# Where a float64 conversion on VectorE keeps its intermediate words: SBUF or a PSUM bank

## The chip, the cores and the metric

One core of one Trainium2 chip runs the whole program. The metric is device time in microseconds, the median of three runs. Engines by their short names: PE (TensorE matmul; PEld its weight load), DVE (VectorE), ACT (ScalarE), POOL (GpSimd), SP (SyncE, which issues most DMAs).

## The reference

Three stages follow one another. The first is attention over 2 batches, 8 heads, 768 positions and 64 columns: each query sees the keys less than 16 positions away and one summary (maximum of the keys, mean of the values) of each block of 32. The second is a dense layer with a gated activation, the third a layer of 8 experts in which every token goes to one expert by a greedy assignment with equal capacity.

```python
scores = concat(where(|i - j| < 16, scale * q @ k.T, -1e9), scale * q @ k_sum.T + log(32))
x = softmax(scores) @ concat(v, v_sum)          # per head, then [1536, 512]
h = x @ w_in                                    # [1536, 2048]
y = (h * clip(h + 3, 0, 6) / 6) @ w_out         # [1536, 512]
assigned = greedy(argsort(-(y @ w_gate)))       # 192 tokens to each of 8 experts
out[mask_e] = relu(y[mask_e] @ w1[e]) @ w2[e]
```

The weights `w_in` and `w_out` reach the core as float64, the rest as float32.

## The kernel before, in words

The 1536 tokens are 12 tiles of 128; three tiles make a unit, so there are four units of 384. Every large matmul runs three times, with operands split into a high part in the fp32r form and the remainder (`WH`, `WL`, `XH`, `XL`).

A float64 weight tile of 128 x 512 arrives as pairs of 32-bit words. DVE turns it into float32 with three integer instructions (`f32_ops`): shift and mask of the upper word, the sign bits or-ed in, the upper bits of the lower word or-ed in. All three write the target tile, and the second and third also read it. For `w_in` these are 16 tiles (`w_conv`, recorded under L268, with the target `win32`, four buffers), for `w_out` again 16 (`fold_take`, under L529, with the target `wout32`, three buffers). Then `w_split` follows: ACT copies the tile into `WH` (L285), POOL subtracts to get `WL` (L286). After its third step a conversion lets SP load the tile four (`w_in`) or two (`w_out`) further on.

`drive` merges generators into one program order by planned shares. Engines run their queues in that order, and semaphores hold an instruction until its operands are there. The stretches in time: a prologue with the attention of unit 0 and the first conversions; layer one of unit 0 (`gemm1`) beside the attention of unit 1 and the other `w_in` conversions; layer one of units 1 and 2 beside the attention of the next unit; layer one of unit 3 beside the `w_out` conversions and their transposes (`out_slice`, `fold_take`, `fold`, which fold the gate's weights into `w_out`); the second layer (`gemm2`) beside the routing; the experts.

PSUM has eight banks, named by number in `bank(i)`. Layer one puts each of the 16 groups of a unit (12 matmuls into one bank, lines 587 to 589) into banks 5 and 6 in turn, and for unit 3 into 5, 6, 2, 3. ACT reads the bank (L590), and then DVE's gate (L601) reads it; after that the bank is free. `turn` transposes the attention weights of a half tile (4 heads), the first half of a tile into bank 2, the second into bank 3 (L404), and ACT copies them out (L406). The preparation of the keys uses banks 2 and 3 as well. In the attention, DVE's small instructions (L382, L394) and its copies of key windows (L354 to L360) have inputs and outputs in SBUF; POOL scales the weights (L396).

The gate of a group is put into the program order after the next group, and behind any conversion that this next group brings.

Of the kernel before, what the change touches and what calls it, by code (L numbers as in the profile page):

```python
# [10 lines left out]
I32 = mybir.dt.int32  # L11
AF = mybir.ActivationFunctionType
OP = mybir.AluOpType
# [14 lines left out]
NU = NT // UT  # L28
U = UT * 128
# [58 lines left out]
def build(ctx, tc, q, k, v, w_in, w_out, w_gate, w1, w2, out):  # L88
    nc = tc.nc
    PE, ACT, DVE, POOL, SP = nc.tensor, nc.scalar, nc.vector, nc.gpsimd, nc.sync  # L90
# [28 lines left out]
    def bank(i):  # L119
        return psum.tile([128, 512], FT, name=f"bank{i}")  # L120
# [107 lines left out]
    win64 = [conv.take([2 * 512], I32) for _ in range(4)]  # L228
    win32 = [conv.take([512]) for _ in range(4)]
    NW = len(win64)  # L230
    wi, wo = w_in.bitcast(I32), w_out.bitcast(I32)

    def f32_ops(dst, src):


        w = src.rearrange("p (f t) -> p f t", t=2)
        d = dst.bitcast(I32)
        return [partial(DVE.tensor_scalar, d, w[:, :, 1], 3, 0x3FFFFFF8, op0=OP.logical_shift_left, op1=OP.bitwise_and),
                partial(DVE.scalar_tensor_tensor, d, w[:, :, 1], -0x40000000, d, op0=OP.bitwise_and, op1=OP.bitwise_or),
                partial(DVE.scalar_tensor_tensor, d, w[:, :, 0], 29, d, op0=OP.logical_shift_right, op1=OP.bitwise_or)]  # L240

    def w_in_load(s):
        SP.dma_start(win64[s % NW].rearrange("p (k f) -> p k f", k=KD),
# [20 lines left out]
            loaded[0] += 1  # L264

    def w_conv(s):
        for op in f32_ops(win32[s % 4], win64[s % NW]):
            op()  # L268
            yield
        if s + NW < NF:  # L270
            soon.append(partial(w_in_load, s + NW))
# [127 lines left out]

    def turn(n, h):  # L400
        A = Abuf[(2 * n + h) % (LAG + 1)]
        p = bank(2 + h)
        for c in range(4):
            PE.transpose(p[:KEYS, c * 128:(c + 1) * 128], A[:, c], ident)  # L404
        at = att.tile([128, 4, 128], FT, name="at", bufs=2)
        ACT.activation(at[:KEYS], p[:KEYS].rearrange("p (c s) -> p c s", c=4), AF.Copy)  # L406
        ats[n, h] = at
# [35 lines left out]
    def halves():  # L443
        for n in range(NT):
# [9 lines left out]
            for h in range(2):  # L454
                t = pend.pop(0) if len(pend) >= LAG else None
                if t:
                    turn(*t)
                    turned.append(t)
                    yield 660
# [26 lines left out]
            if i == 5:  # L486
                while pend or turned:
                    if turned:
                        yield 700
                        values(*turned.pop(0))  # L490
                        yield 1000
                        emit_x()
                    if pend:
                        yield 800
                        t = pend.pop(0)
                        turn(*t)
                        turned.append(t)
                        yield 660
# [26 lines left out]
        SP.dma_start(wout64[f % 2], wo[f * 128:(f + 1) * 128, :])  # L525

    def fold_take(f):
        for op in f32_ops(wout32[f % 3], wout64[f % 2]):
            op()  # L529
        if f + 2 < NF:  # L530
            soon.append(partial(fold_load, f + 2))
# [34 lines left out]
    def out_slice():  # L566

        f = taken[0]
        taken[0] += 1
        if f + 1 < NF:  # L570
            fold_take(f + 1)
        w_split(NF + f, POOL)
        if f % FG == FG - 1:
            fold_pair(f // FG)
# [4 lines left out]
    def gemm1(u, first=False):  # L579
        if u < NU - 1:  # L580
            T[u] = tpool.tile([128, NF, U], FT, name="t")
        xh, xl = (t[u][:, :KD * U].rearrange("p (k s) -> p k s", k=KD) for t in (XH, XL))
        for f in range(NF):
            p = bank((5, 6, 2, 3)[f % (4 if u == NU - 1 else 2)])[:, :U]
            wh, wl = (t[f].rearrange("p (k f) -> p k f", k=KD) for t in (WH, WL))
            for kk in range(KD):
                PE.matmul(p, wh[:, kk, :], xh[:, kk, :], start=kk == 0, stop=False)  # L587
                PE.matmul(p, wh[:, kk, :], xl[:, kk, :], start=False, stop=False)  # L588
                PE.matmul(p, wl[:, kk, :], xh[:, kk, :], start=False, stop=kk == KD - 1)  # L589
            ACT.activation(T[u][:, f, :], p, AF.Relu, bias=three)  # L590
            soon.append(partial(gate, T[u][:, f, :], p))
            if u == NU - 1:
                if (f + 1) * (NF - LEFT) // NF > taken[0]:
                    out_slice()
                if f == EARLY:
                    next(second)
            yield 1950
# [169 lines left out]
    def splits():  # L767
        for s in range(NF + CLAG):
            if s < NF:
                for _ in w_conv(s):  # L770
                    yield 1
            if s >= CLAG:
                w_split(s - CLAG, POOL)
            yield 1
# [4 lines left out]
    for u in range(NU):  # L779
        st = []  # L780
        if u + 1 < NU:
            st = [[attend_unit(u + 1), ATTS[u + 1], -0.02, END[u]]]
            if u == 0:
                st.append([splitting, 4 * (NF - AHEAD) + CLAG, 0.0, S1])
        else:
            actx.close()
            tlast = ctx.enter_context(tc.tile_pool(name="tlast", bufs=1))
            late = ctx.enter_context(tc.tile_pool(name="late", bufs=1))
            T[u] = tlast.tile([128, NF, U], FT, name="t")
            big = late.tile([128, 2 * 2 * 512], I32)  # L790
            wout64 = [big[:, i * 1024:(i + 1) * 1024] for i in range(2)]
            fa = xpool.tile([128, KD * U + 12], FT, name="x")
            wout32 = [fa[:, i * 512:(i + 1) * 512] for i in range(3)]
            fb = xpool.tile([128, KD * U + 12], FT, name="x")
            wt = fb[:, :KD * FG * 128].rearrange("p (k j f) -> p k j f", k=KD, j=FG)
            woy = fb[:, KD * FG * 128:(KD + 1) * FG * 128]
            wg = fb[:, (KD + 1) * FG * 128:(KD + 1) * FG * 128 + KD * 32].rearrange("p (k e) -> p k e", k=KD)
            for f in range(2):
                fold_load(f)
            POOL.memset(wg, 0.0)  # L800
            SP.dma_start(wg[:, :, :E], w_gate.rearrange("(k p) e -> p k e", p=128))
            fold_take(0)
        drive([[gemm1(u), G1, 0, 1]] + st, soon)
# [418 lines left out]
```

## Time and profile before

| | |
|---|---|
| median of three runs | 602.12 us (601.99 to 603.04) |
| the profiled execution | 600.1 us, its span 598.2 us |
| mean granted TensorE clock | 0.981 of full speed |
| PE busy | 551.2 us (92% of the span) |
| DVE busy | 400.6 us (67%) |
| ACT busy | 288.8 us (48%) |
| POOL busy | 178.2 us (30%) |
| chain that ended last | PE 39%, issue 27%, DVE 23%, DMA 4% |

Shares of the whole span are averages over stages that have different limits, so they are a start only. The chain is followed back from the last instruction: its share for DVE is time in which DVE's work was what the next step waited for. The table by stretches of time tells which engine is full where, and the waits tell for whom an engine stood still.

### The profile page before, as it was taken

The page shows a single profiled execution, that of the slowest core. Times are in us where ns is not written, and L with a number is a line of the kernel's source. Part 1 is how long each engine was busy: PE and PEld are TensorE (multiplying, and loading weights), DVE is VectorE, ACT ScalarE, POOL GpSimd, SP SyncE. Part 2 cuts the span into 40 slices and gives each one's busy share as a digit, 9 for nine tenths or more (in the row PEclk, how much of TensorE's full clock was granted, in tenths as well). Part 3 has the DMA queues.
Part 4 walks back from the last instruction along what each step waited for, and adds up shares of the span by engine and source line. Part 5 has one row for each costly group of instructions (what it writes and reads, how often), then busy time and mean ns, then how long its engine had stood idle before and what let it go on. Part 6 is the DMA issues. An engine that isn't in the chain of part 4 may idle for free.

```text
span 598.2 us, 10910 instructions
## 1 busy us (share of the span) xinstructions
PE 551.2 (92%) x3811; PEld 466.8 (78%) x3811; DVE 400.6 (67%) x1215; ACT 288.8 (48%) x694; POOL 178.2 (30%) x204
## 2 busy tenths in 40 slices
PE   7679778989999999899999898899999999999994
PEld 6558667878899999776687676678789889988883
DVE  6898994555534399961037787762588888888880
ACT  4376453435645455641131131133577677776760
POOL 1444648111111034662243434545101101110111
PEclk9879998989999999999999999999999999999998
DMA  9985981202210245330060000003579879887811
GB/s 204 253 194 147 257 200 33 49 18 64 58 39 1 72 142 175 112 93 1 1 201 11 0 2 2 0 19 142 168 219 283 231 241 283 265 253 240 253 61 32
DMA packets 102400, 75.06 MB, mean 125 GB/s; under 512 B 47488, under 2 KB 88448, under 8 KB 101952
## 3 DMA queue, kind: packets, MB, share of 16 engines
q1 hardware_dynamic: 100352, 67.96, 41.8%
q0 software_dynamic: 1984, 6.32, 2.9%
q8 instruction: 32, 0.52, 0.4%
q14 instruction: 32, 0.26, 0.1%
HBM read 67.55 MB, written 6.71 MB: 124 GB/s over the span
## 4 chain that ended last, share of the span: by engine, by line
PE 39%; issue 27%; DVE 23%; DMA 4%; POOL 3%; ACT 2%; SPq 1%; POOLq 0%; ACTq 0%; DVEq 0%
PE bank L587 7%; PE bank L588 6%; PE bank L589 6%; DVE t L268 5%; PE bank L704 3%; PE bank L705 3%; PE bank L706 3%; DVE big L889 3%; POOL out_dram L1025 2%; PE bank L894 2%; DVE x L529 2%; PE bank L613 2%; DMA t<-in_q_dram 2%; PE bank L419 1%; DVE A L380 1%
## 5 line engine op out<-in xcount | busy, mean ns | idle before, releaser
L587 PE MATMUL bank<-x,wh 128*128 128x384 f32 x256 | 92.4, 361 | 9.5 <-DVE t L601 9.3
L295 DVE TENSOR_TENSOR wl<-t,wh 128x1024 fp32r<-128x1024 f32 x64 | 77.0, 1221 | 20.5 <-ACT wh L294 18.1
L681 ACT ACTIVATE work<-t 128x384 fp32r<-128x384 f32 (+2 forms) x80 | 36.4, 459 | 107.5 <-PE bank L705 101.2
L589 PE MATMUL bank<-x,wl 128*128 128x384 f32 x256 | 87.4, 341 | 0.8 <-POOL wl L286 0.8
L588 PE MATMUL bank<-x,wh 128*128 128x384 f32 x256 | 87.1, 340 | 0.8 <-DVE x L77 0.8
L590 ACT ACTIVATE t<-bank,three 128x384 f32<-128x384 f32 x64 | 37.2, 581 | 94.1 <-PE bank L589 94.0
L682 POOL TENSOR_TENSOR tlx<-t,work 128x384 fp32r<-128x384 f32 (+1 forms) x52 | 56.8, 1094 | 84.2 <-ACT work L681 84.2
L704 PE MATMUL bank<-wh,work 128*128 128x512 f32 x192 | 78.0, 406 | 2.0 <-DVE t L601 2.0
L706 PE MATMUL bank<-wh,tlx 128*128 128x512 f32 x192 | 75.3, 392 | 0.1
L705 PE MATMUL bank<-wl,work 128*128 128x512 f32 x192 | 74.8, 390 | 0.0
L1050 PE MATMUL bank<-x,wh 128*128 128x384 f32 x256 | 73.7, 360 | 0.5 <-DVE x L976 0.5
L294 ACT ACTIVATE wh<-t 128x1024 fp32r<-128x1024 f32 x64 | 65.6, 1047 | 0.0
L1052 PE MATMUL bank<-x,wl 128*128 128x192 f32 x256 | 64.2, 251 | 0.0
L601 DVE SCALAR_TENSOR_TENSOR t<-t,bank 128x384 f32<-128x384 f32 x64 | 34.7, 548 | 40.0 <-ACT t L590 40.0
L396 POOL TENSOR_TENSOR A<-A,sm 128x480 f32<-128x480 f32 x24 | 24.2, 1010 | 119.0 <-ACT at L406 74.9
L587 PEld LDWEIGHTS bank<-x,wh 128*128 128x128 f32 x256 | 48.9, 191 | 13.4 <-DVE t L601 5.9
L1025 POOL DMA_INDIRECT out_dram<-t,idx x16 | 14.9, 930 | 141.6 <-DVE t L1074 136.1
L588 PEld LDWEIGHTS bank<-x,wh 128*128 128x128 f32 x256 | 49.1, 192 | 1.4 <-DVE x L77 1.4
L589 PEld LDWEIGHTS bank<-x,wl 128*128 128x128 f32 x256 | 48.9, 191 | 1.2 <-POOL wl L286 1.2
L1052 PEld LDWEIGHTS bank<-x,wl 128*128 128x128 f32 x256 | 48.9, 191 | 0.3
L1066 PE MATMUL bank<-wh,t 128*128 128x512 f32 x128 | 49.0, 392 | 0.0
L1050 PEld LDWEIGHTS bank<-x,wh 128*128 128x128 f32 x256 | 48.1, 188 | 1.2 <-DVE x L976 0.8
(182 smaller groups left out, 1088.9 us busy)
## 6 DMA issues: line engine op xcount, KB each, us to landing
t<-in_moe_w_dram SPq DMA_DIRECT2D x128, 256.0 KB
t<-in_moe_w_in_dram SPq DMA_DIRECT2D x16, 512.0 KB
big<-in_moe_w_out_dram SPq DMA_DIRECT2D x16, 512.0 KB
VW<-in_v_dram SPq DMA_DIRECT2D x20, 192.0 KB
t<-in_v_dram SPq DMA_DIRECT2D x4, 768.0 KB
t<-xs SPq DMA_DIRECT2D x8, 258.0 KB
raw<-in_q_dram SPq DMA_DIRECT2D x8, 256.0 KB
t<-in_k_dram SPq DMA_DIRECT2D x12, 128.0 KB
```

The costliest lines, as they stand in the source:

```text
L294: ACT.activation(hi, x, AF.Copy)
L295: DVE.tensor_tensor(lo, x, hi.bitcast(FT), op=OP.subtract)
L587: PE.matmul(p, wh[:, kk, :], xh[:, kk, :], start=kk == 0, stop=False)
L588: PE.matmul(p, wh[:, kk, :], xl[:, kk, :], start=False, stop=False)
L589: PE.matmul(p, wl[:, kk, :], xh[:, kk, :], start=False, stop=kk == KD - 1)
L682: (DVE if placed[0] else POOL).tensor_tensor(ths[i][1], t, ths[i][0].bitcast(FT), op=OP.subtract)
L704: PE.matmul(acc[j], th[:, c], WH[s], start=f == 0, stop=False)
L705: PE.matmul(acc[j], th[:, c], WL[s], start=False, stop=False)
L706: PE.matmul(acc[j], tl[:, c], WH[s], start=False, stop=f == NF - 1)
L1050: PE.matmul(p, a[:, kk, :], xt[:, kk].rearrange("p c s -> p (c s)"), start=kk == 0, stop=False, skip_group_check=True)
L1052: PE.matmul(p[:, :CAP], b[:, kk, :], xt[:, kk, 0, :], start=False, stop=kk == KD - 1, skip_group_check=True)
L1066: PE.matmul(p, x, w, start=m == 0 and i == 0, stop=m == NM - 1 and i == 2)
```

## The change

The helper `f32_ops` takes a third argument, a bank of PSUM. The first two steps write their words there, the second and third read them from there, and only the third writes the target. Both users pass bank 3. To free that bank, `turn` uses bank 2 for both halves, and layer one of unit 3 rotates over banks 5, 6, 2. Nothing else differs; the same instructions are issued on the same engines in the same order.

```diff
-    def f32_ops(dst, src):
+    def f32_ops(dst, src, mid):
...
-        d = dst.bitcast(I32)
+        o, d = dst.bitcast(I32), mid.bitcast(I32)
         return [partial(DVE.tensor_scalar, d, w[:, :, 1], 3, 0x3FFFFFF8, op0=OP.logical_shift_left, op1=OP.bitwise_and),
                 partial(DVE.scalar_tensor_tensor, d, w[:, :, 1], -0x40000000, d, op0=OP.bitwise_and, op1=OP.bitwise_or),
-                partial(DVE.scalar_tensor_tensor, d, w[:, :, 0], 29, d, op0=OP.logical_shift_right, op1=OP.bitwise_or)]
+                partial(DVE.scalar_tensor_tensor, o, w[:, :, 0], 29, d, op0=OP.logical_shift_right, op1=OP.bitwise_or)]
...
-        for op in f32_ops(win32[s % 4], win64[s % NW]):
+        for op in f32_ops(win32[s % 4], win64[s % NW], bank(3)):
...
-        p = bank(2 + h)
+        p = bank(2)
...
-        for op in f32_ops(wout32[f % 3], wout64[f % 2]):
+        for op in f32_ops(wout32[f % 3], wout64[f % 2], bank(3)):
...
-            p = bank((5, 6, 2, 3)[f % (4 if u == NU - 1 else 2)])[:, :U]
+            p = bank((5, 6, 2)[f % (3 if u == NU - 1 else 2)])[:, :U]
```

## Rows read from the trace of the kernel before

**Rows 1.** Busy us by stretch: length, PE, PEld, DVE, ACT, POOL, clock, DMA, GB/s.
```profile
50.00:95.00 45.00, 34.81 (x302) 30.60 (x294) 43.03 (x97) 23.14 (x65) 24.06 (x17) 1.00 0.77 178
95.00:208.00 113.00, 110.61 (x942) 100.51 (x941) 51.14 (x212) 54.55 (x165) 23.79 (x25) 0.97 0.18 43
208.00:250.00 42.00, 42.00 (x284) 39.98 (x287) 37.79 (x56) 22.55 (x44) 18.02 (x14) 1.00 0.43 145
250.00:265.00 15.00, 12.20 (x83) 9.25 (x81) 13.58 (x16) 7.67 (x16) 11.70 (x13) 1.00 0.41 124
265.00:430.00 165.00, 156.67 (x928) 119.18 (x928) 87.03 (x377) 46.85 (x98) 64.54 (x79) 1.00 0.14 46
```

**Rows 2.** PE's waits, 60 to 100, then 250 to 300: total us, times, longest.
```profile
PE bank L587 <- DVE t L601: 9.3, 6, 2.6
...
PE bank L704 <- DVE t L601: 2.0, 1, 2.0
PE bank L539 <- DVE wgo L553: 0.8, 1, 0.8
```

**Rows 3.** Stretches, DVE's conversions alone (L268 twice, then L529): busy, clock, DMA, GB/s.
```profile
24.00:50.00 26.00, 9.06 (x13) 0.87 0.88 210
50.00:95.00 45.00, 29.39 (x35) 1.00 0.77 178
...
208.00:253.00 45.00, 33.95 (x39) 1.00 0.42 145
```

**Rows 4.** Single lines of the kernel: duration in ns, shortest/median/longest; starts; shapes.
```profile
L268 DVE SCALAR_TENSOR_TENSOR t<-t x32: 662/692/1708, 25.4 to 93.1; 128x512 int32<-128x512 int32 x32
L268 DVE TENSOR_SCALAR t<-t x16: 396/416/1506, 25.0 to 89.5; 128x512 int32<-128x512 int32 x16
...
L601 DVE SCALAR_TENSOR_TENSOR t<-t,bank x64: 536/547/556, 50.4 to 253.4; 128x384 f32<-128x384 f32 x64
```

**Rows 5.** Timeline, POOL and then DVE, 89 to 93 us: start, duration, instruction.
```profile
89.03 4.82 POOL L286 TENSOR_TENSOR wl<-t,wh 128x512 fp32r<-128x512 f32 x3
...
89.54 1.51 DVE L268 TENSOR_SCALAR t<-t 128x512 int32<-128x512 int32 x1
91.08 1.63 DVE L268 SCALAR_TENSOR_TENSOR t<-t 128x512 int32<-128x512 int32 x1
92.64 0.54 DVE L601 SCALAR_TENSOR_TENSOR t<-t,bank 128x384 f32<-128x384 f32 x1
```

**Rows 6.** DVE's groups by line and shape: busy us, mean ns | idle before.
```profile
L682 DVE TENSOR_TENSOR tlx<-t,work 128x256 fp32r<-128x256 f32 x12 | 5.0, 424 | 8.7 <-ACT work L681 8.7
L202 DVE COPY VW<-bank 24x512 f32<-24x512 f32 x8 | 5.1, 689 | 2.3 <-PE bank L198 2.3
L885 DVE SCALAR_TENSOR_TENSOR bank<-bank,inv 128x96 f32<-128x96 f32 x15 | 4.0, 266 | 0.5
L993 DVE TENSOR_TENSOR x<-bank,x 128x256 fp32r<-128x256 f32 x7 | 2.8, 406 | 0.0
```

**Rows 7.** Line 382, a small DVE instruction of the attention, as in rows 4.
```profile
L382 DVE TENSOR_SCALAR sm<-sm x24: 169/280/1112, 11.7 to 190.2; 128x4 f32<-128x4 f32 x24
```

**Rows 8.** Stretches around the end of the loads, as in rows 1.
```profile
82.00:86.00 4.00, 1.88 (x13) 1.60 (x12) 3.97 (x6) 3.57 (x12) 2.02 (x2) 1.00 1.12 217
86.00:90.00 4.00, 3.51 (x21) 2.95 (x19) 3.93 (x9) 1.45 (x3) 1.92 (x2) 1.00 0.04 9
```

**Rows 9.** Stretches around the last input-weight conversion, as in rows 1.
```profile
90.00:94.00 4.00, 1.42 (x21) 1.28 (x21) 3.97 (x4) 0.28 (x1) 3.85 (x3) 1.00 0.00 0
94.00:98.00 4.00, 4.00 (x18) 3.90 (x17) 1.50 (x3) 2.28 (x4) 2.86 (x2) 0.59 0.00 0
```

**Rows 10.** Timeline, end of unit 3's layer one: group 14 on ACT, DVE's gates 14, 15.
```profile
247.56 0.58 ACT L590 ACTIVATE t<-bank,three 128x384 f32<-128x384 f32 x1 [0.56 <-PE bank L589]
...
252.96 1.00 DVE L601 SCALAR_TENSOR_TENSOR t<-t,bank 128x384 f32<-128x384 f32 x2
```

**Rows 11.** Line 406, ACT's copies of the turned halves, as in rows 4.
```profile
L406 ACT ACTIVATE at<-bank x24: 571/577/600, 23.1 to 201.0; 120x512 f32<-120x512 f32 x24
```

## Prediction

> **What bounds the kernel now.** The slices of the page come first, for where PE falls short of full while another engine is full; the table by stretch then makes it exact [rows 1]. From 95 to 208 us PE is busy for 110.6 of 113, from 208 to 250 for 42.0 of 42, from 265 to 430 for 156.7 of 165: PE sets the time there. From 50 to 95 PE has 34.8 of 45 and DVE 43.0; from 250 to 265 PE has 12.2 of 15 and DVE 13.6: there DVE sets it. The waits say what PE lacks [rows 2]: from 60 to 100 the gate of layer one (L601), 9.3 us in six waits, because layer one rotates over two banks and the gate of two groups ago is still queued on DVE; from 250 to 300 the same gate once, 2.0 us, and 0.8 us for a transpose that needs the last converted tile (the profile books it on L553, the copy before it on DVE's queue).
>
> What DVE does there is the conversion: 29.39 us of 45 in 35 instructions [rows 3]. The durations of its line show two populations [rows 4]: TENSOR_SCALAR 396 to 1506 ns around a median of 416, SCALAR_TENSOR_TENSOR 662 to 1708 around 692. The gate, an instruction of the same kind with one input in SBUF and one in a bank, never leaves 536 to 556 ns in 64 calls. The timeline shows why [rows 5]: from 89.03 POOL runs three subtractions back to back for 4.82 us; the conversions that start inside it take 1.51 and 1.63 us, the gate at 92.64, inside it too, 0.54. So a DVE instruction with two SBUF inputs, or one input in the fast copy-like form (416 ns for 512 elements is 0.8 ns each, less than the 1.1 of the others), is held while POOL works, and one with a PSUM operand in place of the second is not.
>
> **The change part by part.** *Conversions.* After it no step has two SBUF inputs, and the first writes PSUM. What this costs undisturbed: the trace has no 512-element shift into a bank, so bounds. A copy of 512 out of a bank took 689 ns, the gate with 384 took 547, that is 1.1 ns for each further element [rows 4, 6].
> First step: low 0.42 (it keeps today's fast form), high 0.78 (the gate's fixed part is 547 - 384 x 1.1 = 125 ns; L885, reading and writing one bank, took 266 ns for 96, so 1.47 ns each if its fixed part is the same, and 512 make 0.88). I take 0.68, near the 512-element copy.
> Second step, in place in the bank: low 0.66 (today's undisturbed), high 0.88 by L885; I take 0.70, since L885's fixed part may be the larger.
> Third step, bank and SBUF to SBUF: the gate's form, 547 + 128 x 1.1 = 0.69.
> Sum 2.07 us a tile, against 1.80 undisturbed today and 2.5 as they ran: the fast form of step one is given up, the holds go.
> From 50 to 95 the 35 instructions are 11 first steps and 12 each of the others: 11 x 0.68 + 12 x 0.70 + 12 x 0.69 = 24.2, so DVE loses 5.2 us; the bounds give 8.9 (24 x 0.66 + 11 x 0.42 = 20.5) and 0.9 (23 x 0.88 + 12 x 0.69 = 28.5). Some holds come back: L382 and its like remain two-port work. L382 lasts between 0.17 and 1.11 us [rows 7], so it is held at times already; POOL is busy for 24.1 of the 45 us [rows 1], and a conversion no longer absorbs the hold ahead of such a call. I add 0.5 (between -1, the holds that L382 has now, and +3, three more of its longest). DVE gains 4.7.
> From 24 to 50 it gains nothing: 13 instructions, 5 x 0.68 + 4 x 0.70 + 4 x 0.69 = 9.0 against 9.06.
>
> A rule of the Trainium skill speaks against it: "VectorE: DVE Perf Modes", section "The TRN2 errata", gives VectorE a fixed part of 58 cycles from SBUF and 120 with a PSUM source, so 65 ns more for each such instruction; by it the two later steps of 12 tiles would take back 24 x 0.065 = 1.6 us of the gain, an estimate from that page. The trace does not agree: a subtraction of 256 elements took 406 ns with a bank as input and 424 with both in SBUF [rows 6]; the sum is made without it.
>
> What is late next in that stretch is a transfer. The input-weight loads and the batch's K and V rows fill the queues: DMA share 1.12 from 82 to 86, 0.04 after [rows 8]. The last conversion starts at 89.54 [rows 5], so if the traffic stayed where it is, it could move forward by 3.5 us at most. The traffic's triggers (the end of a conversion, the attention's progress) move forward too. I take 4.5 us, between 3.5 and 4.7 and nearer the latter; PE's waits of 9.3 us can give that back.
>
> *Clock.* From 90 to 94 PE is busy 1.42 of 4 us at a granted 1.00 (2.4 GHz); from 94 to 98 it is busy throughout at 0.59, part of that at the lower level, 1.2 GHz [rows 9]: 4 x 0.41 = 1.6 us of work not done. The pause before it is the one that shrinks by some 2 us (1.51 + 1.63 for two steps that should take 1.37). From 82 to 86 PE was busy 1.88 of 4 and no fall followed [rows 8]. I take 1.6; bounds 0 and 1.6.
>
> *Unit 3 and what follows.* From 208 to 253, 39 instructions (13 tiles) took 33.95 us [rows 3]; 13 x 2.07 = 26.9, 7 us less, while PE is never idle: worth nothing there. At its end gate 14 starts at 252.96, though its ACT part ran from 247.56 to 248.14 [rows 10]: it stood behind a conversion in DVE's queue. Without the holds it is done before PE asks, and the 2.0 us go; the 0.8 us for the last transposes go too. Bounds 1.0 and 2.8; I take 2.8.
>
> *Three banks in place of four.* PE's group is 42/16 = 2.6 us, so a gate has two groups, 5.2 us, after its own group before its bank is needed, in place of 7.9. Today gate 14 starts 4.8 us late; behind one conversion of 2.07 it starts at most some 2.6 late. Nothing; with holds as today, about 0.1 for the latest gate.
>
> *One bank for the turned halves.* The next half's transposes must wait for the copy out (L406, 0.58 us). The 24 copies lie between 23.1 and 201.0 [rows 11], one in 7.7 us; it is long done. Nothing; with no such cover, 24 x 0.58 = 14 us. The K preparation still uses bank 3, before the first and after the last input-weight conversion, so its order is kept. In a step's own queue nothing is added: the steps stay in DVE's order, and only the last now waits for readers of the target, none of which shows as a wait.
>
> **Sum.** 4.5 + 1.6 + 2.8 = 8.9. The profiled execution took 600.1 (span 598.2), so its like comes to 591.2; the median of the runs shown is 602.12, 2.0 more, and the same sum makes 593.2. Behind each place PE is the bound, so the shift passes to the end.
>
> **The rivals.**
> *All of PE's waits go.* If the gates leave the conversions' shadow altogether, PE wins its 10.2 idle us of 50 to 95 [rows 1], the clock's 1.6 and the 2.8: 587.5. For it: all those waits name the gate. Against: DVE is busy for 43 of 45 us there and loses only 5.
> *The transfers or the remaining two-port calls hold the first stretch.* Then the end of 250 to 265 and about a microsecond remain: 598.3. For it: the share of 1.12, POOL's 24.1 us.
> *The in-place step is slow.* Reading and writing one bank could go at half rate: 512 x 2.08 + 160 = 1.23 us. Then 50 to 95 costs 30.5 + 0.5 against 29.4 (+1.6), 24 to 50 costs 11.1 against 9.1 (+2.0), and nothing comes back at 250, with 0.3 for the three banks: 606.0. It decides from some 1.0 us for that step. Against: L885 took 266 ns for 96, where half rate would make some 350.
> *The change doesn't do what it says.* If POOL holds any DVE access to SBUF, the holds stay and the 16 first steps up to 95 us cost 0.26 more each: 606.3. Against: 64 gates without one hold.
>
> **How the numbers follow.** Forecast 593.2, with 0.56 and a range of its own of 591 to 597; all waits 0.16; first stretch held 0.16; no change 0.04; in-place step 0.04; holds stay 0.04. A measurement can tell 0.2%, 1.2 us, from no change. Faster: 0.56 + 0.16 + most of the third, 0.87 in all; same 0.05; slower 0.08. The range reaches from 587.0 (most of the second) to 599.5 (nearly all of the third); with the tails of these two, no change and the two slower cases it leaves out about 0.2.
>
> **What would show it.** Right: the conversion's line without a tail, steps at 0.65 to 0.8 us whatever POOL does, POOL's subtractions shorter than the 1.6 us each that they took beside the conversions (4.82 for three) [rows 5]; PE's wait on L601 from 60 to 100 halved, the one at 250 gone; the clock at 1.00 after the last conversion. Wrong: conversions still over 1 us beside POOL (then the holds have another cause); an idle time of DVE ended by the input-weight DMA; new waits of L587 on L601 between 208 and 250 (the third bank was needed); L382 and the window copies taking over the holds.

## The result and the profile after

The changed kernel's median is 596.50 us over 4 runs, against 602.58 for the kernel before beside it: ratio 0.9892, 95% interval 0.9863 to 0.9921. A second set of 6 runs gave 596.58, ratio 0.9894 (0.9849 to 0.9938). The profiled execution took 597.2 (span 595.4). So 6.1 us went, where 8.9 were forecast; the time lies in the range and 3.3 us above the forecast. Medians are of all runs, ratios of the undisturbed ones alone: one of the 12 runs of the scratch-tile version below took 883.17 us at a mean granted clock of 0.558.

First the steps themselves. The view of single lines of the changed kernel (duration in ns, shortest/median/longest) answers to [rows 4]:

```profile
L268 DVE TENSOR_SCALAR bank<-t x16: 672/686/699, 25.0 to 92.7; 128x512 int32<-128x512 int32 x16
L268 DVE SCALAR_TENSOR_TENSOR bank<-t,bank x16: 671/696/696, 25.7 to 93.4; 128x512 int32<-128x512 int32 x16
L268 DVE SCALAR_TENSOR_TENSOR t<-t,bank x16: 657/686/690, 29.9 to 94.5; 128x512 int32<-128x512 int32 x16
...
L286 POOL TENSOR_TENSOR wl<-t,wh x16: 1264/1289/1302, 41.1 to 96.3; 128x512 fp32r<-128x512 f32 x16
```

The tail is gone: no step of the input weights is longer than 699 ns, where two-input steps had reached 1708, and none of the output weights (L529) is longer than 720, where 1782 had been reached. POOL's subtraction has lost its tail too: 1302 ns at most, while the kernel before shows up to 1777 for it:

```profile
L286 POOL TENSOR_TENSOR wl<-t,wh x16: 1272/1476/1777, 39.3 to 95.1; 128x512 fp32r<-128x512 f32 x16
```

The timeline (start, duration, instruction) has the same overlap as [rows 5] had, POOL first and then DVE:

```profile
92.58 3.79 POOL L286 TENSOR_TENSOR wl<-t,wh 128x512 fp32r<-128x512 f32 x3
...
92.67 0.69 DVE L268 TENSOR_SCALAR bank<-t 128x512 int32<-128x512 int32 x1
93.39 0.70 DVE L268 SCALAR_TENSOR_TENSOR bank<-t,bank 128x512 int32<-128x512 int32 x1
...
94.46 0.68 DVE L268 SCALAR_TENSOR_TENSOR t<-t,bank 128x512 int32<-128x512 int32 x1
```

All three steps now run inside POOL's three subtractions at their own length. The stretches (length; busy PE, PEld, DVE, ACT, POOL; granted clock; DMA share; GB/s) answer to [rows 1]:

```profile
50.00:95.00 45.00, 38.38 (x314) 33.24 (x315) 38.19 (x104) 25.25 (x73) 19.99 (x17) 0.96 0.81 191
208.00:250.00 42.00, 41.66 (x274) 39.03 (x274) 33.81 (x57) 21.87 (x43) 15.57 (x13) 1.00 0.46 154
250.00:265.00 15.00, 15.00 (x103) 12.08 (x103) 7.50 (x14) 10.12 (x20) 11.84 (x15) 1.00 0.34 98
```

From 50 to 95 DVE has fallen from 43.0 to 38.2 us and is no longer full, yet PE still lacks 6.6. From 208 to 250 PE lacks 0.3, one wait for the gate that was not there before; from 250 to 265 it is full. The waits of 60 to 100 name what remains, PE's first and DVE's second, as in [rows 2]:

```profile
PE bank L587 <- DVE t L601: 4.9, 4, 2.2
...
DVE bank L268 <- DMA t<-in_moe_w_in_dram: 2.3, 1, 2.3
```

PE's wait for the gate is halved in this profile (a second profile of the changed kernel, below, has 8.1 us), and DVE itself waits, which it did not do in the profile before. The chain of waits, in order of time, shows the load; the timeline below it shows the instruction that it held:

```profile
67.41 10.67 DMA t<-in_moe_w_in_dram
```

```profile
78.10 0.69 DVE L268 TENSOR_SCALAR bank<-t 128x512 int32<-128x512 int32 x1 [2.25 <-DMA t<-in_moe_w_in_dram]
```

This is the eleventh input-weight tile. SP issued its load at 67.41, behind batch 1's K and V rows, and it landed 10.67 us later. In the profile before, the eleventh conversion began at 74.53, 10.8 us after SP came to its load at 63.73, and showed no wait: the load had fitted under the slow conversions. It had little or no room there: of the kernels below that keep the input weights' words in SBUF with POOL's subtractions in place, all three wait for this same tile, 0.15, 0.80 and 0.95 us.

The place where PE begins the K transposes of batch 1 (L318) closes the front. It lies at 102.48 us before and 102.27 after. The first layer-one matmul, however, came at 46.56 before and at 50.66 after. Both kernels run the same instructions up to the first conversion, which starts at 24.96 and at 24.99 us; by then the granted clock was back at 1.00 in the profile before, while in the profile after it stayed at 0.50, the lower level of 1.2 GHz, until 32 us. The stretch from 20 to 34 us, before and then after, as in [rows 1]:

```profile
20.00:34.00 14.00, 11.29 (x136) 9.21 (x138) 12.22 (x42) 7.98 (x30) 5.87 (x8) 0.87 1.13 272
20.00:34.00 14.00, 14.00 (x112) 11.95 (x112) 9.32 (x33) 5.83 (x23) 5.48 (x7) 0.56 1.03 253
```

This is luck of the execution: the second profile of the changed kernel has 0.81 in the same stretch and its first layer-one matmul at 48.40. From the one mark to the other it is 55.9 us before and 51.6 after, 4.3 less. From the last L419 of the attention to the first matmul of layer two (L704) it is 50.61 and 49.25, and from there to the first L613 17.65 and 16.66: together 2.4 less. Everything behind is the same to 0.2 us (327.0 and 326.9). So the two profiled executions, 2.9 us apart, hide part of the gain behind the luck of the start, and the medians, 6.1 apart, agree with 4.3 + 2.4 within their interval. The 4.3 is the number of one pair: between the two marks, the kernels below with the input weights' words in SBUF and POOL's subtractions have 55.5 to 58.0 us, and all four profiles with these words in the bank and the same loads 51.2 to 54.0.

### The profile page after: what moved, and what is told of

Read it like the earlier page. It is cut to its first block, busy times and chain, and to the rows that moved or that the text cites. A ratio compares the mean times of both kernels' runs of the same rounds, so it can differ in the third digit from the quotient of the medians.

```text
span 595.4 us, 10943 instructions
## 1 busy us (share of the span) xinstructions
PE 554.4 (93%) x3811; PEld 469.4 (79%) x3811; DVE 384.4 (65%) x1215; ACT 288.7 (48%) x694; POOL 170.2 (29%) x204
## 4 chain that ended last, share of the span: by engine, by line
PE 43%; issue 26%; DVE 18%; DMA 5%; POOL 3%; ACT 2%; SPq 1%; POOLq 0%; DVEq 0%; ACTq 0%
PE bank L587 7%; PE bank L588 6%; PE bank L589 6%; PE bank L704 4%; PE bank L705 3%; PE bank L706 3%; DVE big L889 3%; POOL out_dram L1025 2%; PE bank L894 2%; DVE bank L268 2%; PE bank L419 2%; PE bank L613 2%; DMA t<-in_moe_w_in_dram 2%; DMA t<-in_q_dram 2%; PE bank L372 2%
## 5 line engine op out<-in xcount | busy, mean ns | idle before, releaser
L587 PE MATMUL bank<-x,wh 128*128 128x384 f32 x256 | 92.5, 361 | 6.6 <-DVE t L601 5.1
L704 PE MATMUL bank<-wh,work 128*128 128x512 f32 x192 | 78.1, 407 | 0.0
L587 PEld LDWEIGHTS bank<-x,wh 128*128 128x128 f32 x256 | 48.7, 190 | 11.5 <-DVE t L601 4.3
```

The costliest lines, as they stand in the source:

```text
L704: PE.matmul(acc[j], th[:, c], WH[s], start=f == 0, stop=False)
```

## The experiments

All ratios are against the kernel before on the same chip, with 95% intervals. Edits are shown against the changed kernel, in the run without POOL's subtractions against the kernel before.

**The bank edits alone.**

```diff
-        for op in f32_ops(win32[s % 4], win64[s % NW], bank(3)):
+        for op in f32_ops(win32[s % 4], win64[s % NW], win32[s % 4]):
...
-        for op in f32_ops(wout32[f % 3], wout64[f % 2], bank(3)):
+        for op in f32_ops(wout32[f % 3], wout64[f % 2], wout32[f % 3]):
```

> The three bank edits alone (one bank for the turned halves, three banks for unit 3's layer one); the words stay in the target tile in SBUF. Theory (POOL holds every conversion step that has two SBUF inputs or the fast one-input form, and the bank removes that): nothing is gained, 602.0 to 603.5, the conversion line keeps its tail up to 1.7 us, the wait of layer two for the gate at about 250 stays near 2 us. Rival (the banks' new layout is part of the gain): 600 or less. Rival (the third bank for layer one was needed): over 603.5 and new waits of L587 on L601 between 208 and 250.

604.50 us, ratio 1.0025 (0.9999 to 1.0052). Steps up to 1706 ns. PE's waits from 200 to 250:

```profile
PE bank L587 <- DVE t L601: 1.5, 2, 0.9
```

Before, there was none there. So the fourth bank was in use as long as the conversions were held: the waits that the second rival names came, 1.5 us of them, and the median is over its 603.5, though the interval just includes no change. The front's and the end's waits stayed (8.6 and 2.0 us). Of the gain, nothing comes from the layout.

**A scratch tile in SBUF instead of the bank, input weights.**

```diff
+    words = att.tile([128, 512], FT, name="words")
...
+        for op in f32_ops(win32[s % 4], win64[s % NW], words):
...
+        for op in f32_ops(wout32[f % 3], wout64[f % 2], wout32[f % 3]):
```

> As the changed kernel for the input weights, but the intermediate words lie in a scratch tile in SBUF, not in a bank; the output-weight conversions keep their words in the target. Theory of the held port: the two later steps still have two SBUF inputs, so no gain: 602 to 603.5, steps up to 1.7 us beside POOL, PE waits some 9 us for the gate between 60 and 100. Rival (the gain comes from freeing the target tile: only the last step waits for its readers): the front gains as in the changed kernel, 597 to 599.

605.40 us, ratio 1.0056 (1.0024 to 1.0088). The steps of the input weights (one line lower in this kernel):

```profile
L269 DVE TENSOR_SCALAR words<-t x16: 396/426/1386, 26.5 to 93.4; 128x512 int32<-128x512 int32 x16
L269 DVE SCALAR_TENSOR_TENSOR words<-t,words x16: 664/692/1664, 27.0 to 94.8; 128x512 int32<-128x512 int32 x16
L269 DVE SCALAR_TENSOR_TENSOR t<-t,words x16: 661/692/1579, 30.2 to 96.9; 128x512 int32<-128x512 int32 x16
```

The order of the writes and the freed target are those of the changed kernel, and the tail is back in all three steps. So not the separate place for the words, but its being a bank, takes the holds away. Freeing the target gains nothing. The time lies above the 602 to 603.5 expected; the layout's waits, 1.5 us here too, are part of that, and the rest is open.

**One half of the conversions each.** The input weights alone keep their words in the bank (`f32_ops(wout32[f % 3], wout64[f % 2], wout32[f % 3])` for the others), then the output weights alone, the other way round.

> Words in the bank for the input weights alone, all bank edits kept. Theory: the front's part of the gain, 3.5 to 6 us (597 to 599); no step of L268 over 0.75 us; PE's wait for the gate from 60 to 100 about 5 instead of 9.3; the 2.0 us wait at 250 stays. If the front's gain is eaten by the load of the eleventh input-weight tile, DVE waits about 2 us for it and the front's gain is nearer 3.5.

599.96 us, ratio 0.9944 (0.9913 to 0.9974), just outside what was expected; the third bank's waits, 1.5 us in this profile too, which the expectation had forgotten, are enough to account for it. PE's wait from 60 to 100 is 5.8, DVE waits 1.9 for the eleventh tile, L318 begins at 101.91, the 2.0 us at 250 stay.

> Words in the bank for the output weights alone, all bank edits kept. Theory: the waits at 250 and 264 go, 2.8 us, nothing else: 599.3 to 600.3; no step of L529 over 0.75 us, L268 keeps its tail. Rival (with three banks the gain at 250 is given back as waits between 208 and 250): 601.5 or more.

600.32 us, ratio 0.9930 (0.9896 to 0.9964); L529's steps take at most 711 ns, L268's up to 1701, and from 250 to 300 PE has no wait on DVE left. Against the layout alone the halves are worth about 0.8% and 0.95%, within some 0.4% each; both count, and their sum, 1.8%, agrees with the 1.3% between the layout alone and the changed kernel only loosely.

**Without POOL's subtractions.**

```diff
-        lo.tensor_tensor(WL[s], x, WH[s].bitcast(FT), op=OP.subtract)
+        ACT.activation(WL[s], x, AF.Copy)
```

> The kernel before, with POOL's subtraction after each conversion replaced by a plain copy on ACT (the low parts of both dense layers' weights are then not remainders; this part of the computation is left out). Words stay in SBUF. Theory (it is POOL's work that holds the steps): L268 and L529 lose their tail, steps 0.40 to 0.45 and 0.66 to 0.72 us, except beside POOL's scaling of the attention weights, where up to 1.0 more is left for a few; PE's wait for the gate from 60 to 100 falls below 6 us and the one at 250 goes; ACT has 32 x 0.6 us more. 595 to 600. Rival (the tail comes from DVE itself, from reading the words with a stride or from rewriting the target in place): the tail stays.

596.47 us, ratio 0.9884 (0.9863 to 0.9905): as much as the change, with words in SBUF and four banks. From 208 to 253 the 39 instructions took 24.68 us in place of 33.95 [rows 3], 1.90 a tile, and PE has no wait on DVE between 200 and 300. In the front the picture is mixed. POOL, now free early, begins batch 1's block sums (L186) at 89.19, and they hold the last steps as the subtractions had; the eleventh tile is late by 3.1 us. POOL and then DVE on the timeline:

```profile
89.19 11.09 POOL L186 TENSOR_TENSOR t<-t 96x1024 f32<-96x1024 f32 x8
...
89.70 2.58 DVE L268 TENSOR_SCALAR t<-t 128x512 int32<-128x512 int32 x1
92.31 1.63 DVE L268 SCALAR_TENSOR_TENSOR t<-t 128x512 int32<-128x512 int32 x1
```

Here even the first step, one input and one output in SBUF in the fast form, is held for over 2 us by another POOL instruction. So POOL is the holder, whichever of its SBUF instructions runs. PE's waits for the gate in the front stayed at 9.0, where less than 6 was expected, and the front at 56.5 us: from 50 to 95 us the 36 instructions took 26.44 us, less than before but more than the changed kernel's 24.61, and DVE stood still for the load besides. The load and the block sums took the place of the subtractions. This profiled execution, 598.98 us, is the slowest of the four.

**The late load.** In the changed kernel, batch 1's V rows for the block sums go one attention tile later; in the next run the K rows too.

```diff
                     for j in range(4):
                         load_rows("kraw", k, b + 1, j)
+                if h == 0 and i == 5 and b + 1 < B:
                     for g in range(2):
                         vsum_load(b + 1, g)
```

> The changed kernel, the two loads of batch 1's V rows for the block sums (1.5 MB together) issued one attention tile later, so that the input-weight loads go ahead of them. Theory (the front's gain is cut by the load of the eleventh input-weight tile, which stands behind K and V): DVE's wait of 2.25 us for it falls below 0.7, the stretch from the first layer-one matmul to the first K transposes of batch 1 falls from 51.6 by 1 to 2.2 us, the time by as much against the changed kernel (594 to 595.5). Rival (the wait is hidden by something else in that stretch): same stretch within 0.5 us. Risk: the block sums on POOL start late and PE waits for them near 125.

594.34 us, ratio 0.9863 (0.9839 to 0.9886). DVE has no wait for the load, and from the first layer-one matmul to the K transposes it is 49.27 us, 2.3 less.

> As the run before, but batch 1's K rows too go one tile later and the V rows one and a half. Theory: the wait for the eleventh tile goes wholly; the stretch is 49.4 to 50.6 us long unless the K rows are late, which would show as a wait of L318 on their load. 593.5 to 595.5.

595.71 us, ratio 0.9874 (0.9854 to 0.9894); the stretch is 49.25 us, without a wait for the K rows; both lie just outside what was expected. Nothing beyond the V rows' part.

The version with late V rows was run again beside the changed kernel:

> The changed kernel once more, as a base for the two beside it. 594.5 to 598, ratio 0.987 to 0.992; DVE's wait for the eleventh input-weight tile about 2 us again; the stretch from the first layer-one matmul to the first K transposes of batch 1 51 to 52 us.

596.58 us (594.99 to 598.0), and 1.8 us of wait for the eleventh tile in one piece. This execution started layer one at 48.40 us, 2.3 earlier than the first profile, and reached L318 at 102.37, as late as that: PE waited 8.1 us for the gate on the way. So the stretch was 54.0 us, longer than expected.

> The changed kernel with batch 1's V rows for the block sums loaded one tile later, once more. Theory (the transfer cut the front's gain): faster than the changed kernel beside it by 1.5 to 2.5 us, 592.5 to 596, the stretch 49.3 us. Rival (what is won there is lost to the clock or to later waits): within 0.6 us of it.

594.41 us (592.3 to 596.13), ratio 0.9858 (0.9813 to 0.9904): 2.2 below the changed kernel beside it, as expected, though the ranges overlap; the first time it was 2.2 as well, against runs of another set. DVE again has no wait for the load. The stretch was 50.23 us, 0.9 longer than expected and 3.7 shorter than beside it.

In four profiles of kernels with the input weights' words in the bank and the loads as they were, L318 begins at 102.27, 102.37, 101.91 and 102.03, while their first layer-one matmul ranges from 48.40 to 50.82. With the late V rows it begins at 98.54 and 100.28, with the K rows late too at 102.32 and in the next experiment at 100.61, always 49.25 to 50.23 us after the first layer-one matmul. A front whose end stays put while its start moves by 2.4 us, and which follows its start when a load goes later, is paced by the load. That the end stays put rests on one execution, for three of the four starts lie within 0.4 us; that DVE's wait goes when the V rows go is shown.

**The query rows first.** As the last, and the second tile's query rows ahead of batch 0's V rows.

> As the run beside it, and the query rows of the second tile are loaded ahead of batch 0's V rows for the block sums in place of behind them. PE waits 3.3 to 6.3 us for these rows near 16 to 20 us in the profiles so far, and the granted clock is at its lower level after that wait for a time that differs from run to run. Theory (that wait starts the low clock): the wait shrinks below 2.5 us, the first layer-one matmul starts at 45 to 49 instead of 48 to 53 us, 590 to 594. Rival (the block sums, now later by the time of 256 KB, hold PE instead, at line 198): same time within 1 us.

594.71 us, ratio 0.9868 (0.9820 to 0.9916): the rival. PE's wait for the rows (5.2 us beside it) is gone, PE waits at L198 instead, and the first layer-one matmul came at 51.34, later than the 45 to 49 expected; the view of PE's waits from 10 to 60:

```profile
PE bank L198 <- POOL t L186: 2.9, 1, 2.9
...
PE bank L198 <- DVE t L183: 2.3, 1, 2.3
```

The clock's dip follows the pause: 18 to 26 us in the run beside it, 22 to 34 here.

**Two banks for unit 3.**

```diff
-            p = bank((5, 6, 2)[f % (3 if u == NU - 1 else 2)])[:, :U]
+            p = bank((5, 6)[f % 2])[:, :U]
```

> The changed kernel with two banks for unit 3's layer one in place of three. A gate then has one group, 2.6 us, before its bank is needed. Theory: with steps of 0.7 us the gate is behind at most one conversion, so waits appear but small: L587 on L601 from 208 to 250 between 2 and 6 us in all, 598 to 602. If three banks had no slack left, the waits with three (0.3 us) would already be near those with two.

598.72 us, ratio 0.9918 (0.9883 to 0.9953); L587 waits 1.9 us once, just below what was expected. So with short steps, three banks cost 0.3 us of waits and two 1.9; the times do not tell the two apart.

## Why the prediction was right, and where it was off

- *The holds and the steps: right.* Forecast 0.68, 0.70 and 0.69 us, measured means 0.686, 0.692 and 0.682. From 50 to 95 us 36 instructions, twelve tiles, took 24.61 us, 2.05 a tile (forecast 2.07; 2.5 before). The two experiments that tell the cause apart, a scratch tile in SBUF (tail stays) and no subtraction on POOL (tail goes, except beside other POOL work), both came out for POOL as the holder. The Trainium skill states a rule that explains this ("SBUF — State Buffer", section "SBUF: two separate sides"): DVE in a two-port mode or with two SBUF inputs and GpSimd take a shared pair of ports in turn, each for a whole instruction. The traces agree: a four-element L382 still takes up to 1100 ns in the changed kernel. The other rule of the Trainium skill, which the prediction set aside, 65 ns more for each instruction with a PSUM source, is not seen: 0.682 and 0.692 us against an undisturbed 0.692 with two SBUF inputs.
- *Holds that come back: within the bounds, the size not settled.* For 50 to 95 us 0.5 more was forecast. L382's four calls there took 2.24 us before and 2.03 after, but 3.95 in the second profile of the changed kernel; the copies of key windows at L354 fell from 1.69 to 0.60.
- *The front: the mis-sized term.* 4.5 us of work and 1.6 of clock were forecast, 6.1 in all; the pair of profiles gives 4.3. DVE's work did shrink, but the eleventh tile's load stopped it for 2.25 us, one of the signs that the prediction itself had named against it. It had named transfers as next, but took its bound from the last conversion (3.5 us of room) and let the traffic move with its triggers. The tile that mattered was the first one behind K and V, and it had next to no room. Moving those V rows took DVE's wait away and gave 2.2 us beside the changed kernel.
- *The clock: wrong.* After the last conversion it stays at 1.00, as forecast. But a pause earlier takes the fall over. From the stretches of the changed kernel, as above:

```profile
66.00:70.00 4.00, 1.75 (x12) 1.50 (x11) 3.83 (x9) 3.57 (x12) 1.27 (x1) 0.98 0.97 237
70.00:74.00 4.00, 4.00 (x28) 3.36 (x27) 3.76 (x9) 1.10 (x2) 1.19 (x2) 0.59 1.03 247
...
96.00:100.00 4.00, 4.00 (x38) 3.71 (x36) 1.11 (x2) 1.82 (x4) 3.97 (x3) 1.00 0.01 2
```

  PE is busy for 1.75 of 4 us, then 4 us are at 0.59: 1.6 us of work, as much as in [rows 9], in another place. That it cost the front time there is not shown: of the two runs of the version with late V rows alone, one has such a fall from 68 to 72 us, with PE waits of 3.8 us for the gate and a front of 49.27 us, the other has none between 50 and 100 us, with waits of 4.9 us for the gate and 1.2 for ACT, and a front of 50.23. So whether the 1.6 us belonged into the sum stays open.
- *Unit 3's end: right.* Both waits went; 2.4 us of the 2.8 came, the rest went partly to the third bank's 0.3.
- *Three banks: right with short steps, wrong with held ones.* "About 0.1" was forecast for holds as today; it is 1.5. The estimate took gate 14, 4.8 us late, for the latest gate, and the mean group of 2.6 us; in the trace before, gate 2 starts 5.65 us after its ACT part, and the first three groups begin 2.1 us apart. In the layout run groups 4 and 5 wait for gates 1 and 2. Nor does a gate start at most 2.6 late with short steps, as the prediction says: gate 2 is 4.43 late in the changed kernel, and the one wait of 0.3 us, another of the signs that the prediction had named, is for it.
- *One bank for the turned halves: right.* No profile shows a wait of L404 for ACT.

Of the rivals, the held first stretch (598.3 us, 0.16) came nearest: the time is 1.8 us from it and 3.3 from the forecast, so the number alone speaks rather for the rival. The parts speak for the forecast: the front gave 4.3 us in the pair of profiles, and the input weights' half 4.5 against the layout alone, where the rival has about one. All waits gone (587.5), the slow in-place step and the unchanged holds are out.

**What stays open.** Executions of one and the same kernel differ by several us (the kernel before: 597.97 to 607.16), and the profiles show the low clock between 18 and 50 us in different places. How much of the spread that makes was not isolated. Conversions without POOL beside them and with the V rows late were not tried together. Nor were the late V rows in the kernel before: as its relatives waited for the same tile by up to 0.95 us, part of the 2.2 us may not need the change.

**The best version run.** The changed kernel with batch 1's V rows one tile later: 594.34 and 594.41 us, below both kernels here.

## What to carry to other kernels

Look at the longest durations of a DVE line beside its median, and lay POOL's timeline over them: where two-input SBUF instructions are stretched and those with a PSUM operand are not, an intermediate that moves to a free bank takes the stretch away, though it gives up the fast one-input form (0.42 to 0.69 us here). Before counting such a gain, look at each transfer that the sped-up engine consumes and compare issue-to-use times one by one: the smallest slack decides, and it stood at the first tile behind a burst of other loads. A pause removed in one place can reappear in another, and the clock's fall with it; whether that fall costs anything has to be read there too.

## What the runs showed of the hardware beyond that

In the changed kernel the third step starts 0.80 us after the second, which takes 0.69 (66.97 and 67.77 us), while before, two steps ran back to back in 1.42. It is not the bank that sets them apart: with the scratch tile in SBUF it is the same 0.80 us (64.97 and 65.77), and the second step, which also takes words from the bank, starts 0.03 us after the first. What these two kernels share is that the last step alone writes the target and waits for its readers; that this is the reason is argued, not shown. POOL gains too when DVE stops asking: its 512-element subtraction fell from a median of 1476 to 1289 ns.
